# Row swaps of each batch's last two rows moved from DMA to VectorE, and ones products ahead of the first input on TensorE

**Chip, cores, metric.** One core of one Trainium2 chip. The time is the device time of one execution in microseconds (us); quoted times are medians of the fast runs, and lower is better.

## The reference

A Fourier mixing layer is followed by a two-layer network on all 24,064 tokens.

```python
X = np.fft.rfft(x, axis=1)                 # x: 8 batches x 3008 x 256
Yr = Xr @ w_r - Xi @ w_i + b_r             # mixing of the spectrum
Yi = Xr @ w_i + Xi @ w_r + b_i
Yr, Yi = soft_threshold(Yr), soft_threshold(Yi)      # lam = 0.01
y = np.fft.irfft(Yr + 1j * Yi, n=3008, axis=1)
h = np.maximum(y @ w_in, 0)                # 256 -> 2048
out = (s * h * h + b) @ w_out              # 2048 -> 256
```

## The kernel before

Transforms are products with tables: 3008 = 94 x 32 is done in two steps. Batch 0 has its own code (`first_batch`), which has nothing to hide behind. Batches 1 to 7 are transformed in small units, woven between the network's products of earlier batches. A unit of the middle steps handles one of 12 "rows" i (two pairs of spectrum blocks). Between mixing and the inverse transform, a row's 64-partition halves must change places; this is the swap. An *eviction* is the instruction of VectorE or ScalarE that copies a product's result out of its PSUM bank, so that TensorE can use the bank again; the *squaring* (`gt<-rt`) is the h * h of the network.

```python
# batches 1 to 7, row i of 12 (H = 12)
def mix_unit(i):
    ps = one_bank()                                   # one of two PSUM banks "psf"
    ...                                               # 4 products
    t, m = ring[0][:, i % 4], ring[0][:, 4 + i % 2]
    nc.vector.tensor_tensor(out=t, in0=ps, in1=..., op=ALU.add)      # the mixing sum; frees the bank
    nc.vector.tensor_tensor(out=m, in0=t, in1=low, op=ALU.max)
    nc.vector.tensor_tensor(out=m, in0=m, in1=high, op=ALU.min)
    nc.vector.tensor_tensor(out=t, in0=t, in1=m, op=ALU.subtract)
    z = ring[0][:, 6 + i % 6]
    for j in range(2):
        for r in range(2):
            nc.sync.dma_start(                        # the swap: 4 transfers of 32 KB
                out=z[64 * r : 64 * r + 64, j], in_=t[64 * j : 64 * j + 64, r]
            )

def inv_unit(i):                                      # inverse transform of row i
    ps = one_bank()
    for j in range(2):
        nc.tensor.matmul(ps[:, j, :], T_t[:, 2 * i + j, :], z[:, j, :], start=True, stop=True)
    ...

# batch 0
def first_batch():
    for c in range(4):                                # four pieces of x, as they land
        for dc in range(2):
            ...                                       # 8 products; ScalarE and VectorE evict to ut
    place_f(); place_t()                              # tables F_t, F_2, T_t copied from F_c, T_c
    gate = nc.gpsimd.tensor_copy(out=w_in_t[0][0:1, 0:1], in_=T_c[0:1, 0, 0:1])
    with tc.issue_after(gate.ins):                    # GpSimd: waits until T_c has landed
        emit_load_x(1)
        emit_load_weights()
    for i in range(...):
        mix(i); fwd_dft(i - 1); inv_dft(i - 2)        # ... and the rest of the transform
        if i == 6:
            make_w_g(); make_bounds()                 # arithmetic on GpSimd
```

## Time and profile before

| | before |
|---|---|
| median (lowest to highest, 4 runs) | 873.02 us (872.90 to 874.69) |
| span of the profiled execution | 871.1 us |
| TensorE, VectorE, ScalarE busy | 96%, 80%, 74% |
| idle of TensorE between 100 and 850 us | 8.6 us, of which 7.6 waits for swaps |
| stretches at half clock (granted clock 0.50) after 100 us, while TensorE works | 2, of 3.41 us each (127.19 to 130.61 and 236.42 to 239.84) |

A product's line in the timeline shows its start, its length, how many products were merged, and in brackets how long TensorE had been idle and what ended that. TensorE's busy share says how often it had work, not how fast it did it: the same four products take 0.60 us at full clock and 1.06 at half. The lines themselves stand in the prediction.

### The profile page before, as it was taken

To read this page: it belongs to the slowest core of one execution; us is meant where nothing else is said; L and a number is where in the kernel's file an instruction comes from. 1 tells how busy PE (TensorE), PEld (TensorE's weight loads), DVE (VectorE), ACT (ScalarE), POOL (GpSimd) and SP (SyncE) were. 2 spreads that over 40 slices of the span, in tenths; PEclk is the share of its full clock that TensorE was granted. 3 is DMA by queue.
4 is the path that set the end of the run, shared out by engine and by line. 5 is a ranking of instruction groups with operands and counts; after the bars stand their busy time and mean duration, and the time that the engine had idled before them with its cause. 6 is when DMAs were issued, how large, how long until landed. Compare 5 with 4: busy or idle time off the path is not lost.

```text
span 871.1 us, 16955 instructions
## 1 busy us (share of the span) xinstructions
PE 838.8 (96%) x6580; PEld 599.4 (69%) x6580; DVE 693.4 (80%) x971; ACT 640.7 (74%) x848; POOL 32.8 (4%) x53
## 2 busy tenths in 40 slices
PE   4889999999899999999999999999999999999996
PEld 3757766777567766777667776777667777766665
DVE  6788977888778987888878988798877887776664
ACT  4687876787677886787777787787877778666662
POOL 4100000000000000000000000000000000000000
PEclk9999999999999999999999999999999999999999
DMA  8754366423664248522764236633364133411111
GB/s 187 130 120 119 90 156 160 140 57 81 163 147 133 79 107 226 135 65 74 175 165 121 68 94 168 168 92 85 86 189 120 50 86 103 116 31 38 37 39 53
DMA packets 109346, 96.90 MB, mean 111 GB/s; under 512 B 10318, under 2 KB 101714, under 8 KB 107922
## 3 DMA queue, kind: packets, MB, share of 16 engines
q1 hardware_dynamic: 103266, 81.41, 32.6%
q0 software_dynamic: 6000, 14.42, 10.2%
q8 instruction: 51, 0.84, 0.4%
q14 instruction: 29, 0.24, 0.1%
HBM read 52.54 MB, written 46.66 MB: 114 GB/s over the span
## 4 chain that ended last, share of the span: by engine, by line
PE 89%; DMA 5%; ACT 2%; DVE 2%; issue 1%; SPq 1%; POOL 0%; DVEq 0%; POOLq 0%
PE psh L689 36%; PE psa L758 36%; PE psf L558 4%; DMA ring<-ring 3%; PE psf L493 3%; PE psf L529 2%; PE psf L544 2%; PE psf L638 2%; PE psf L585 2%; DMA x<-in_x_dram 1%; ACT rt L696 1%; DVE T_t L291 1%; PE psh L357 1%; ACT yt L158 0%; ACT m L393 0%
## 5 line engine op out<-in xcount | busy, mean ns | idle before, releaser
L696 ACT ACTIVATE rt<-psh 128x1024 f32<-128x1024 f32 (+2 forms) x384 | 386.8, 1008 | 121.3 <-PE psh L689 119.6
L703 DVE TENSOR_TENSOR gt<-rt 128x1024 f16<-128x1024 f32 (+2 forms) x322 | 385.8, 1200 | 111.2 <-ACT rt L696 110.7
L758 PE MATMUL psa<-w_out_t,gt 128*128 128x256 f16 (+1 forms) x3024 | 455.5, 273 | 0.1
L758 PEld LDWEIGHTS <-gt 128*128 128x128 f16 (+1 forms) x3024 | 301.7, 101 | 188.3 <-issue 3.6
L689 PE MATMUL psh<-yt,w_in 128*128 128x512 f16 (+1 forms) x1344 | 398.5, 379 | 0.0
L689 PEld LDWEIGHTS <-w_in 128*128 128x128 f16 x1536 | 143.2, 98 | 26.0 <-issue 1.1
L768 DVE SCALAR_TENSOR_TENSOR ost<-psa,s_bc,bias_bc 128x512 f32<-128x512 f32 (+1 forms) x96 | 70.8, 737 | 8.9 <-PE psa L758 6.1
L158 ACT CAST v<-psf 128x512 f16<-128x512 f32 x79 | 46.0, 582 | 29.0 <-PE psf L585 28.4
L700 ACT ACTIVATE gt<-rt 128x1024 f16<-128x1024 f32 (+2 forms) x62 | 65.4, 1055 | 0.9
L563 DVE TENSOR_TENSOR ring<-psf,s 128x512 f16<-128x512 f32 x84 | 57.4, 683 | 3.4 <-PE psf L558 3.3
L158 ACT CAST u<-psf 96x512 f16<-96x512 f32 x79 | 45.7, 580 | 16.5 <-PE psf L493 16.2
L158 ACT CAST xf<-psf 128x512 f16<-128x512 f32 x78 | 45.7, 585 | 10.4 <-PE psf L529 10.4
L689 PE MATMUL psh<-tail,w_in 128*128 128x512 f16 (+1 forms) x192 | 52.1, 353 | 0.0
L558 PE MATMUL psf<-W_g,xf 128*128 128x256 f16 x336 | 50.4, 273 | 0.0
L158 ACT CAST yt<-psf 128x480 f16<-128x480 f32 (+2 forms) x71 | 36.4, 526 | 10.8 <-PE psf L638 10.7
L493 PE MATMUL psf<-x,A_t 94*96 94x512 f16 x104 | 39.9, 384 | 1.1 <-ACT yt L158 0.5
L585 PE MATMUL psf<-ring,T_t 128*128 128x256 f16 x168 | 33.2, 275 | 7.7 <-DMA ring<-ring 7.6
L569 DVE TENSOR_TENSOR ring<-ring,high 128x512 f16<-128x512 f16 x84 | 35.5, 422 | 2.1
L570 DVE TENSOR_TENSOR ring<-ring 128x512 f16<-128x512 f16 x84 | 35.4, 422 | 2.0
L568 DVE TENSOR_TENSOR ring<-ring,low 128x512 f16<-128x512 f16 x84 | 35.3, 420 | 1.5
L558 PEld LDWEIGHTS <-xf 128*128 128x128 f16 x336 | 32.9, 98 | 3.7
L182 POOL DMA_DIRECT2D x<-in_x_dram x32 | 16.7, 525 | 492.3 <-PE psf L493 456.0
(77 smaller groups left out, 479.3 us busy)
## 6 DMA issues: line engine op xcount, KB each, us to landing
out_dram<-ost SPq DMA_DIRECT2D x152, 128.0 KB
x<-in_x_dram POOLq DMA_DIRECT2D x32, 376.0 KB, 6.4
ud<-u SPq DMA_DIRECT2D x28, 384.0 KB
us<-ud SPq DMA_DIRECT2D x28, 384.0 KB
ring<-ring SPq DMA_DIRECT2D x336, 32.0 KB
vd<-v SPq DMA_DIRECT2D x42, 256.0 KB
vs<-vd SPq DMA_DIRECT2D x14, 768.0 KB
out_dram<-ost SPq DMA_DIRECT2D x16, 120.0 KB
```

Of the source, the lines that this page charges most:

```text
L158: return None, nc.scalar.copy(out=dst, in_=src)
L493: nc.tensor.matmul(ps[0:96, :], A_t[0:N1, :], x16[(b, c)][0:N1, j * D : (j + 2) * D], start=True, stop=True,)
L558: nc.tensor.matmul(ps[:, r, :], xt[:, 2 - r, dc], W_g[:, dc, r], start=(dc == 0), stop=(dc == DC - 1),)
L563: nc.vector.tensor_tensor(out=t, in0=ps, in1=hold[i // 2][:, i % 2].unsqueeze(1).to_broadcast([P, 2, D]), op=ALU.add,)
L569: nc.vector.tensor_tensor(out=m, in0=m, in1=high, op=ALU.min)
L585: nc.tensor.matmul(ps[:, j, :], T_t[:, 2 * i + j, :], z[:, j, :], start=True, stop=True)
L689: nc.tensor.matmul(o, w_in_t[dc][:, mc * P : (mc + 1) * P], r, start=(dc == 0), stop=(dc == DC - 1),)
L696: nc.scalar.activation(out=rt[:, :, 0:w], in_=ps[:, :, 0:w], func=AF.Relu)
L700: nc.scalar.activation(out=gt[:, :, 0:w], in_=rt[:, :, 0:w], func=AF.Square)
L703: nc.vector.tensor_tensor(out=gt[:, :, 0:w], in0=rt[:, :, 0:w], in1=rt[:, :, 0:w], op=ALU.mult)
L758: nc.tensor.matmul(ps[0:size, h, :], gts[(ti, mc // 2)][:, mc % 2, sub * size : (sub + 1) * size], w_out_t[:, mc, :], start=(mc == 0), sto ...
L768: nc.vector.scalar_tensor_tensor(out=ost[0:size, 0:k], in0=ps[0:size, 0:k], scalar=s_bc[0:size], in1=bias_bc[0:size, 0:k], op0=ALU.mult, o ...
```

## The change

It has two parts. The swaps of rows 10 and 11, at the end of a batch, become VectorE copies. And TensorE multiplies a tile of ones while the pieces of the first x arrive, which is meant to have it at full clock when real work comes.

```diff
+    ones = cpool.tile([P, P], F16, name="ones")      # moved up
+    nc.vector.memset(ones, 1.0)
+    def keep_awake(n):
+        ps = other_bank()
+        for _ in range(n):
+            nc.tensor.matmul(ps[:, 0:P], ones, ones, start=True, stop=True)
 ...
     def first_batch():
+        keep_awake(44)
         for c in range(N2 // XCH):
             for dc in range(DC):
 ...
-                    nc.tensor.matmul(
+                    last_pe = nc.tensor.matmul(
 ...
+            with tc.issue_after(last_pe.ins):
+                keep_awake(18 if c < 3 else 12)
 ...
             for j in range(2):
                 for r in range(2):
-                    nc.sync.dma_start(
-                        out=z[64 * r : 64 * r + 64, j], in_=t[64 * j : 64 * j + 64, r]
-                    )
+                    o, a = z[64 * r : 64 * r + 64, j], t[64 * j : 64 * j + 64, r]
+                    if i < H - 2:
+                        nc.sync.dma_start(out=o, in_=a)
+                    else:
+                        nc.vector.tensor_copy(out=o, in_=a)
+                        load["dve"] += 0.13
```

`load` is the counter by which the kernel, while it is built, shares evictions between VectorE and ScalarE. The line numbers of the kernel move: the inverse product L585 is L598 after, L689 is L702, L758 is L771, and the new copy is L590.

More of the change, by code (lines that the diff above doesn't have):

```diff
@@ L244 @@
     nc.vector.memset(neg_lam, -LAM)
-    ones = cpool.tile([P, P], F16, name="ones")
-    nc.vector.memset(ones, 1.0)
     F_t = cpool.tile([P, NPAIR, P], F16, name="F_t")
```

## The prediction

> **What bounds the kernel now.** I read the page's busy shares first, then the waits, then the timeline of TensorE around each long wait, then the first 30 us on TensorE and VectorE, and last the busy times by stretch.
>
> ```profile
> PE 838.8 (96%) x6580; PEld 599.4 (69%) x6580; DVE 693.4 (80%) x971; ACT 640.7 (74%) x848; POOL 32.8 (4%) x53
> ...
> 100.00:850.00 750.00, 741.38 (x5708) 526.90 (x5706) 604.43 (x839) 563.41 (x737) 16.42 (x26) 1.00 0.42 110
> ...
> PE psf L585 <- DMA ring<-ring: 7.6, 6, 3.2
> ```
>
> TensorE (PE) is busy 96% of the span. From 100 to 850 us it idles only 750.00 - 741.38 = 8.6 us, and 7.6 us of that is one kind of wait: the inverse transform (L585) waiting for the swap of its rows, the ring<-ring transfers, 6 times, 3.2 us at the longest. Everything else in that stretch is hidden behind TensorE; VectorE (DVE) has 750 - 604 = 146 us to spare. The six waits stand in the timeline at 126.43 (2.06 us), 236.05 (3.18), 327.59 (1.21), 432.47 (0.30), 536.17 (0.48) and 536.81 (0.36): sum 7.59. Each is before the last inverse product of a batch, row i = 11 of 0 to 11 (at 432 and 536 one of its two products); batches 6 and 7 have none.
>
> The waits cost more than their length. The longest:
>
> ```profile
> 232.27 0.60 PE L758 MATMUL psa<-w_out_t,gt 128*128 128x256 f16 x4
> 236.05 0.63 PE L585 MATMUL psf<-ring,T_t 128*128 128x256 f16 x2 [3.18 <-DMA ring<-ring]
> 236.48 1.06 PE L689 MATMUL psh<-yt,w_in 128*128 128x512 f16 x2
> 237.33 1.06 PE L758 MATMUL psa<-w_out_t,gt 128*128 128x256 f16 x4
> ...
> 240.52 0.60 PE L758 MATMUL psa<-w_out_t,gt 128*128 128x256 f16 x4
> ...
> 127.20:130.60 3.40, 3.40 (x14) 1.97 (x13) 0.46 (x1) 1.74 (x3) 0.00 (x0) 0.50 0.79 208
> ...
> 236.40:239.80 3.40, 3.40 (x12) 1.68 (x13) 0.69 (x1) 0.68 (x2) 0.00 (x0) 0.50 0.47 146
> ```
>
> The same four products take 0.60 us before the wait and 1.06 after it, until about 239.8. The stretches just behind the two longest waits have a granted clock of 0.50 and carry 12 and 14 products where the 3.4 us after them carry 25. After the 1.21 us wait nothing of the kind shows: the stretch 325.2 to 328.6, where it lies, has TensorE busy 2.19 of 3.40 us (64%), and the products after it are at 0.60 again. In the two stretches before the slow ones TensorE was busy 1.34 of 3.40 (39%) and 0.33 of 3.40 (10%).
>
> The start:
>
> ```profile
> 14.29 1.46 PE L320 MATMUL psh<-A_t,x 94*128 94x96 f16 x16 [1.20 <-DMA x<-in_x_dram]
> ...
> 21.39 0.80 PE L357 MATMUL psh<-W_t,ut 128*128 128x256 f16 x3 [1.10 <-ACT g L364]
> 24.43 0.26 PE L388 MATMUL psf<-g,F_t 128*128 128x128 f16 x1 [2.25 <-DVE g L367]
> 24.50 0.31 PE L388 MATMUL psf<-g,F 128*128 128x128 f16 x1
> 24.60 0.31 PE L388 MATMUL psf<-g,F_t 128*128 128x128 f16 x1
> ...
> 16.93 0.25 DVE L285 COPY F<-F_c 64x384 f16<-64x384 f16 x1
> ...
> 18.47 4.65 DVE L291 COPY T_t<-T_c 32x1536 f16<-32x1536 f16 x4
> 23.16 1.23 DVE L367 TENSOR_TENSOR g<-psh,b_g 128x1024 f16<-128x1024 f32 x1
> ```
>
> Starts of 128-column products lie 107 ns apart at 24.5 us, and 55 ns apart from about 29 us. So TensorE runs slowly until about 28 us, though the page's clock row shows 9 there; the durations decide. But TensorE isn't what bounds this stretch. The x pieces land at 6.2, 9.1, 11.6 and 14.3 us; from 15.65 to 24.4 VectorE works with no idle (last two ut evictions, eight F copies, four T_t copies, first g), and the first forward product waits for that g.
>
> [...]107 against 55 ns, and two slow stretches whose ends in the timeline lie some 3.4 us apart. [...]The trace has the 64x384 copies at 0.25 us each, starting about 0.17 us apart, so I take 0.16 us of engine time per new copy and about 0.25 us for the last to be visible. [...]the chain's swaps take 4.4 to 7.7 us here, behind other traffic, so a copy on chip is far shorter.
>
> **Part 1, the swaps.** Rows 10 and 11 of each of 7 batches take 4 transfers each: 56 of 336 leave the queue and become 56 VectorE copies of 64x256 f16. VectorE gains 56 x 0.16 = 9 us, spread over seven places, 1.3 us each, against 146 us spare: nothing on the path. Is the copy early enough? In batch 2 the last mixing product starts at 222.05, VectorE ends that row's subtraction at 226.76, and four copies make it about 227.6 with completion. The product that waited was ready at 232.87, so 5 us remain. In batch 1 the mixing product is at 117.1 and the inverse is ready at 124.4, similar. So all six waits should go: 7.6 us. The two half-clock stretches go with them: 3.41 us each at half speed cost 3.41 x 0.5 = 1.71 us each, 3.4 us together. Nothing hides this, because TensorE has no other idle in this stretch to swallow it. Sum: 11.0 us. I take off 0.4 us for leftover short waits, since the balance counter now shifts some evictions between the engines.
>
> **Part 2, the ones products.** The ones tile is set first on VectorE (0.17 us at about 0.9), so 44 products can start at about 1.15 us. At 107 ns they last 4.7 us, until 5.9, just before x at 6.2. With the following 18 per piece (1.9 us slow, 1.0 fast) the array should run at full clock by about 8 us. They cost nothing: after the fast 16 products (about 0.7 us) and 18 more (1.0), 1.7 of the roughly 2.6 us between pieces is filled. What does it buy? ScalarE's eviction of the last piece starts 0.85 us after the piece's first product, 8 x 80 ns + about 0.2; at full clock 8 x 42 ns (the pitch of the 96-column products at 42 us) + 0.15 = 0.49. So VectorE's chain starts, and all behind it ends, 0.36 us sooner. The 16 mix products then take 1.8 instead of 3.4 us, but only to wait for VectorE: 12 extra products end before 16 us, mixing ends at about 18.3, and until about 24.1 TensorE has 3 products to do. That is almost 6 us with some 0.3 us of work, more idle than the 2.06 us that dropped the clock at 126. So I expect it slow again at 24 us, and warmed again by real work as before, at 27 to 30 us. If it stayed fast, the 4.5 us from 24.4 would shrink by at most 2.3, and VectorE and ScalarE would give some back: 1 to 2 us. I weigh that 1 in 6 and take 0.5 us for the whole part.
>
> Sum: 873.0 - 11.0 + 0.4 - 0.5 = **861.9 us**, 1.3% less.
>
> **Rivals.** (a) *The wait moves.* Row 9 still goes by transfer, and its inverse at 229.44 has no wait but perhaps little room: its issues end at 222.2, and a swap like row 11's 7.7 us would land at 229.9. For: the slack is thin in batch 2. Against: nothing before row 9 gets faster within its batch, and the queue holds fewer transfers. It would give back 1 to 3 us: 863 to 865. (b) *VectorE becomes the bound.* Copies stand in line ahead of the squaring and the output evictions. For: 80% busy. Against: no product waits for gt at all now, and 1.3 us per batch is one squaring (1.2 us). Cost under 2 us: up to 864. (c) *The transfers were hidden anyway*, the 3% that the chain of waits gives to ring<-ring being flight time beside which TensorE worked. True of most of that 3% (26 us), but the 7.6 us are real idle, so I don't count the 26. If another transfer (vd to vs, x) fell due in the same place, only the clock penalty would go: 869. Nothing waits for vs or us now. (d) *The start gains more*: 859.5 to 860.5. (e) *The ones products are in the way*: if the array is still slow at the first piece, 16 x 80 + 18 x 107 ns = 3.2 us outlasts the 2.9 us to the next piece by 0.3 us; later pieces catch up.
>
> **Range and chances.** (a) and (b) pull up by 1 to 3 us, (d) down by 1.5 to 2.5[...]. Hence 859.5 to 865.5. Faster by over 2% needs 17.5 us, more than all idle and slow clock that I can find on the path: 2%. Slower by over 2% has no mechanism of that size: 1%. Within 2%: 97%.
>
> **What would show it.** Right: no wait of L585 for ring transfers; no stretch at clock 0.50 between 100 and 850 us; VectorE up by some 9 us; copies of 64x256 at 0.2 to 0.25 us; last-piece eviction 0.3 to 0.4 us sooner; 128-column products again 107 ns apart at 24 us, the T_t copies again ahead of the first g. Wrong: waits at row 9, or products waiting for VectorE; or 55 ns already at 24 us, which would mean the start gained more than I say.

Passages that no trace of this case shows are cut out at the marks. No term of the sum is among them: 873.0 - 11.0 + 0.4 - 0.5 = 861.9. The pulls that stand give 859.4 (861.9 - 2.5) to 864.9 (861.9 + 3). The 107 and 55 ns behind the first mark are the distances between starts of 128-column products given before it. "Full clock by about 8 us" is the author's estimate; in the trace before, products that started in a row from 24.43 us on were at full pace by 29.09.

## The result

| | before | after |
|---|---|---|
| median (lowest to highest, 4 runs each) | 873.02 (872.90 to 874.69) | 861.36 us (860.90 to 862.33) |
| span of the profiled execution | 871.1 | 860.5 us |
| VectorE busy | 693.4 | 699.4 us |
| TensorE idle, 100 to 850 us | 8.6 | 1.4 us |

The ratio is 0.9863, 95% interval 0.9846 to 0.9881. A ratio here is the mean time of one kernel's fast runs over that of the other's fast runs of the same rounds, so it is not quite the ratio of the medians. The predicted time was 861.9.

First the middle stretch of the changed kernel, busy time by engine (TensorE, weight loads, VectorE, ScalarE, GpSimd, then granted clock, DMA share, GB/s), and the same for the two 3.4 us stretches which in the kernel before held the longest wait and the half clock behind it:

```profile
100.00:850.00 750.00, 748.59 (x5803) 535.24 (x5800) 619.08 (x897) 572.66 (x753) 16.87 (x26) 1.00 0.41 108
...
233.00:236.40 3.40, 3.40 (x25) 2.18 (x24) 2.77 (x3) 2.29 (x3) 0.00 (x0) 1.00 0.35 95
236.40:239.80 3.40, 3.40 (x26) 2.30 (x24) 2.66 (x3) 2.23 (x4) 0.51 (x1) 1.00 0.98 253
```

No wait for a swap is left, and no half clock from 100 us to the end of TensorE's work. The place that waited 3.18 us before is a smooth run now; these are its inverse products in TensorE's timeline:

```profile
228.89 0.38 PE L598 MATMUL psf<-ring,T_t 128*128 128x256 f16 x2
229.97 0.38 PE L598 MATMUL psf<-ring,T_t 128*128 128x256 f16 x2
```

And these are the end of the last row's arithmetic and its copies in VectorE's timeline:

```profile
224.57 0.42 DVE L580 TENSOR_TENSOR ring<-ring 128x512 f16<-128x512 f16 x1
225.02 0.97 DVE L590 COPY ring<-ring 64x256 f16<-64x256 f16 x4
```

The copies end at 226.0, 4 us before row 11's product needs them.

**Where the time came from.** I cut the traces at marks that both kernels have, the start of the first product of the network, the last inverse product of each batch (where a line of TensorE's timeline merges its two products, the start of that line) and the end of the last product. Intervals in us:

| interval up to | before | before, 2nd trace | after | after, 2nd trace |
|---|---|---|---|---|
| first product of the network | 56.60 | 58.85 | 57.98 | 56.83 |
| end of batch 1 | 71.46 | 71.53 | 68.86 | 68.87 |
| batch 2 | 107.99 | 108.69 | 103.13 | 103.14 |
| batch 3 | 91.54 | 91.10 | 88.34 | 88.33 |
| batch 4 | 104.88 | 104.90 | 104.83 | 104.82 |
| batch 5 | 104.34 | 104.67 | 103.14 | 103.15 |
| batch 6 | 99.65 | 99.65 | 99.62 | 99.62 |
| batch 7 | 101.18 | 101.18 | 101.18 | 101.17 |
| last product | 126.94 | 126.94 | 126.94 | 126.94 |

From the first product of the network on, the change saves 11.9 us in the first pair of traces, all of it in the intervals with waits and half clock. What follows batch 7 is the same to 0.01 us. The start is another matter: it varies by over 2 us from run to run, and in these traces the change does not clearly shorten it.

### The profile page after: what moved, and what is told of

The parts are those of the page before. It is cut to its first block, busy times and chain, and to the rows that moved or that the text cites. A ratio compares the mean times of both kernels' runs of the same rounds, so it can differ in the third digit from the quotient of the medians.

```text
span 860.5 us, 17125 instructions
## 1 busy us (share of the span) xinstructions
PE 839.1 (98%) x6690; PEld 604.3 (70%) x6690; DVE 699.4 (81%) x1019; ACT 642.8 (75%) x856; POOL 33.2 (4%) x53
## 4 chain that ended last, share of the span: by engine, by line
PE 89%; DVE 4%; ACT 3%; DMA 2%; issue 1%; SPq 0%; POOL 0%; DVEq 0%; POOLq 0%
PE psh L702 36%; PE psa L771 36%; PE psf L568 4%; PE psf L503 3%; PE psf L539 2%; PE psf L554 2%; PE psf L598 2%; PE psf L651 2%; DMA x<-in_x_dram 1%; DVE gt L716 1%; ACT rt L709 1%; PE psh L367 1%; DVE T_t L298 1%; ACT yt L158 1%; ACT m L403 0%
## 5 line engine op out<-in xcount | busy, mean ns | idle before, releaser
L771 PE MATMUL psa<-w_out_t,gt 128*128 128x256 f16 (+1 forms) x3024 | 453.9, 272 | 0.1
L771 PEld LDWEIGHTS <-gt 128*128 128x128 f16 (+1 forms) x3024 | 301.1, 101 | 186.9 <-issue 1.7
L702 PE MATMUL psh<-yt,w_in 128*128 128x512 f16 (+1 forms) x1344 | 396.9, 378 | 0.0
L702 PEld LDWEIGHTS <-w_in 128*128 128x128 f16 x1536 | 142.8, 98 | 26.6 <-issue 1.7
L573 DVE TENSOR_TENSOR ring<-psf,s 128x512 f16<-128x512 f32 x84 | 57.4, 683 | 3.5 <-PE psf L568 3.3
L158 ACT CAST xf<-psf 128x512 f16<-128x512 f32 x82 | 48.0, 585 | 11.1 <-PE psf L539 11.1
L702 PE MATMUL psh<-tail,w_in 128*128 128x512 f16 (+1 forms) x192 | 52.1, 353 | 0.0
L158 ACT CAST yt<-psf 128x480 f16<-128x480 f32 (+2 forms) x76 | 38.5, 518 | 14.4 <-PE psf L651 14.4
L651 PE MATMUL psf<-C_t,vs 96*128 96x96 f16 x448 | 32.9, 205 | 0.0
```

The lines of the kernel that those rows point to most:

```text
L158: return None, nc.scalar.copy(out=dst, in_=src)
L573: nc.vector.tensor_tensor(out=t, in0=ps, in1=hold[i // 2][:, i % 2].unsqueeze(1).to_broadcast([P, 2, D]), op=ALU.add,)
L651: nc.tensor.matmul(ps[:, j * 96 : (j + 1) * 96], vs[(b, h)][:, k, ec * P : (ec + 1) * P], C_t, start=True, stop=True,)
L702: nc.tensor.matmul(o, w_in_t[dc][:, mc * P : (mc + 1) * P], r, start=(dc == 0), stop=(dc == DC - 1),)
L771: nc.tensor.matmul(ps[0:size, h, :], gts[(ti, mc // 2)][:, mc % 2, sub * size : (sub + 1) * size], w_out_t[:, mc, :], start=(mc == 0), sto ...
```

## Experiments

Twelve kernels, in three groups of four; those of a group ran on one chip beside the kernel before, whose medians there were 873.67, 873.32 and 873.98 us. All gave the right result.

### 1. Each part alone

`swaps_only` is the change without all `keep_awake` calls; `awake_only` has them but leaves every swap a transfer:

```diff
# swaps_only
-        keep_awake(44)
-            with tc.issue_after(last_pe.ins):
-                keep_awake(18 if c < 3 else 12)
# awake_only
-                    if i < H - 2:
+                    if i < H:
```

> Only the swaps of rows 10 and 11 go to VectorE; no ones products. Theory (nearly all of the gain is the six waits, 7.6 us, and the two half-clock stretches behind them, 3.4 us): 873.0 - 11.0 = 862.0 us, within 1 us of the full change (861.4), no half-clock stretch after 100 us. Rival (the ones products at the start carry a part of the gain worth naming, 2 us or more): 863.5 us or above.

Measured: 862.06 us, ratio 0.986 (0.9836 to 0.9883).

> Only the ones products at the start; all swaps stay transfers. Theory (VectorE's copies bound the start, the clock falls back before 24 us): 872 to 873.5 us, the six kinds of wait for the ring transfers still there, and 128-column products again 107 ns apart at 24 us. Rival (the faster start is a gain in itself): 871 us or below.

Measured: 874.57 us, ratio 0.9988 (0.9961 to 1.0016). Its trace has 7.5 us of waits for swaps, in 8 pieces, and two half-clock stretches after 100 us.

So the swaps carry the whole change within what these runs resolve; the ones products alone are worth nothing measurable. `awake_only` came out 1.1 us above its expected range, with an interval that still holds 1. Its profiled run had a late start: one of VectorE's F copies lasted 2.80 us, and the first forward product came at 27.02 (section 4 has more of this).

### 2. What a wait costs beyond its length

The first attempt filled the wait instead of removing it: 32 ones products just ahead of row 11's inverse in batches 1 and 2 of the kernel before.

```diff
# fill_waits, on the kernel before
             z = zt.pop(i)
+            if i == H - 1 and b <= 2:
+                for _ in range(32):
+                    nc.tensor.matmul(ps[:, 0, 0:P], ones, ones, start=True, stop=True)
```

> The kernel before, with 32 products of the ones tile (128 columns, about 1.8 us at full clock) put ahead of the last inverse product in batches 1 and 2 only, into the bank that this product then overwrites. They lie inside the two longest waits, so the wait for the transfer stays and only its idle time is filled. Theory (a long wait is paid twice, the second time as 3.41 us at half clock): both half-clock stretches vanish and the time falls by 2 x 1.71 = 3.4 us to 869.6 us, although the transfers land no sooner. Rival (the half clock is hidden, or the products cost what they save): 872.5 to 874 us.

Measured: 872.43 us, ratio 0.998 (0.9958 to 1.0002): between the two theories, and not clear of zero. The trace shows that the experiment was built on an error of mine. In batch 1 the wait is not row 11's:

```profile
125.25 0.27 PE L588 MATMUL psf<-ring,T_t 128*128 128x256 f16 x1
127.59 0.28 PE L588 MATMUL psf<-ring,T_t 128*128 128x256 f16 x1 [2.07 <-DMA ring<-ring]
...
128.80 1.95 PE L586 MATMUL psf<-ones 128*128 128x128 f16 x32
130.59 0.38 PE L588 MATMUL psf<-ring,T_t 128*128 128x256 f16 x2
```

L588 is the inverse product here. TensorE waited between the two products of row 10, and the ones products came after, in front of row 11, where they only cost 1.8 us. In batch 2 they stood in the right place: no idle was left there, and no half clock followed. The trace goes further with the theory than the time does: no half clock is left after 100 us, and from the first product of the network to the end of the last product it takes 804.67 us, against 807.98 and 808.65 in the two traces of the kernel before. But in batch 1 the half clock is gone although the wait stayed, and the intervals of the times hold both no gain and the whole 3.4 us. One hit and one miss cannot settle the sum.

The next experiment, made for another question, answered it. `row11_only` is the full change with `if i < H - 1`: row 10's swaps stay transfers.

> The full change with row 11 alone copied by VectorE, row 10 left as transfers. Theory (all six waits were for row 11): the same as the full change within 1 us, 860.5 to 862.5 us. Rival (row 10's transfers are next in line and become the wait, as its inverse stands just ahead of row 11's): a wait of L598 for ring transfers appears, 1 to 5 us worse, with perhaps a half-clock stretch.

Measured: 868.29 us, ratio 0.9932 (0.9913 to 0.9952), some 7 us above the full change. The theory fell, and the rival was right and even too mild. There is one wait, row 10's in batch 1. TensorE's timeline:

```profile
130.27 0.39 PE L598 MATMUL psf<-ring,T_t 128*128 128x256 f16 x1 [3.77 <-DMA ring<-ring]
130.45 0.63 PE L503 MATMUL psf<-x,A_t 94*96 94x512 f16 x1
130.88 1.06 PE L702 MATMUL psh<-yt,w_in 128*128 128x512 f16 x2
```

Two half-clock stretches lie around and behind it (busy times by stretch, columns as above):

```profile
128.60:132.00 3.40, 1.73 (x6) 0.84 (x7) 0.00 (x0) 1.07 (x2) 0.00 (x0) 0.50 0.81 254
132.00:135.40 3.40, 3.40 (x14) 1.91 (x13) 0.93 (x2) 1.02 (x1) 0.00 (x0) 0.50 0.31 101
135.40:138.80 3.40, 3.40 (x25) 2.32 (x24) 1.91 (x2) 1.79 (x3) 0.00 (x0) 1.00 0.56 132
```

Batches 1 and 2 together take 74.09 + 104.78 = 178.87 us here and 68.87 + 103.14 = 172.01 in the second trace of the full change: 6.9 us for one wait. Of it 3.77 is the idle time. From 130.27, where work resumes, to 135.39, where the clock comes back, 5.1 us pass at half speed, worth 2.6 us. That leaves 0.5 us. A part of it is idle which the profile does not show: a product of 256 columns is drawn 0.27 us long but the next starts 0.11 us later, so some 0.16 us of every wait counts as busy. Here the wait is seen to be paid a second time with nothing else changed: the second payment is some two thirds of the first.

### 3. How many rows VectorE can take

```diff
# all_rows: if i < 0      # rows8_11: if i < H - 4
```

> The full change with all 12 rows of each batch copied by VectorE, 336 copies, no ring transfers. By the 0.22 us per copy of the changed kernel's trace, at most 62 us more of VectorE than with 56 copies, less what the balance counter moves to ScalarE: VectorE from 81% to about 87%. Theory (the copies lie in VectorE's spare time as long as it has some): 860.5 to 863 us, no wait of L598. Rival (VectorE in line order delays the squarings and evictions that TensorE needs): products of L771 or L702 wait for VectorE, 866 us or more.

Measured: 878.81 us, ratio 1.0049 (1.0027 to 1.0071), 17.7 us slower than the full change on the same chip. I had expected no loss, and the rival was right about the time, though the products that wait are not those it named. VectorE is at 85%, short of full. TensorE's timeline, with one of its new waits:

```profile
291.43 0.60 PE L568 MATMUL psf<-W_g,xf 128*128 128x256 f16 x4
...
295.57 0.60 PE L554 MATMUL psf<-W_t,xf 128*128 128x256 f16 x4 [1.58 <-DVE ring L573]
```

VectorE's work in the same moments:

```profile
292.53 0.93 DVE L590 COPY ring<-ring 64x256 f16<-64x256 f16 x4
293.49 1.23 DVE L716 TENSOR_TENSOR gt<-rt 128x1024 f16<-128x1024 f32 x1
294.63 0.28 DVE L545 TENSOR_TENSOR xf<-xf 128x256 f16<-128x256 f16 x1
294.83 0.68 DVE L573 TENSOR_TENSOR ring<-psf,s 128x512 f16<-128x512 f32 x1
```

And the largest group of these in the view of waits (total, times, longest):

```profile
PE psf L554 <- DVE ring L573: 5.6, 10, 1.6
```

The mixing products at 291.43 are done by 292.03, but their sum L573, which empties the bank, starts at 294.83, behind four copies, a squaring and an addition. Meanwhile the next row's products (L554) find no free psf bank, and TensorE idles. So what counts is not VectorE's mean load but how long a bank waits in its line. TensorE's idle from 100 to 850 us is 11.4 us there, 10.0 more than in the full change; the rest of the 17.7 us is not accounted for.

> The full change with rows 8 to 11 copied (112 copies instead of 56). With all rows copied, TensorE waited for VectorE's mixing sums, which stood behind the copies and held the two mixing banks; it cost 17 us. If that cost is in proportion to the extra copies (17 us for 280 more), 56 more cost 3.5 us: 864 to 865.5 us. If there is a threshold of VectorE's load below which the copies are free: 861 to 862.5 us.

Measured: 864.35 us, ratio 0.9894 (0.9873 to 0.9916). So the step from 56 to 112 copies is not free: it costs some 3 us, as the proportion to `all_rows` said. Whether the first 56 cost anything was not tested. Two waits for L573 stand in the trace (0.84 and 1.26 us). By copied rows per batch the times are 868.3 (one), 861.1 to 861.4 (two), 864.4 (four) and 878.8 (twelve), so two is the best of those tried. Fewer leaves a transfer late, more makes banks wait.

### 4. What sets the start

`after_again` is the full change once more; the other two edit it.

```diff
# pool_later: GpSimd's second set of work waits for the T_t copies, not for their source
-        gate = nc.gpsimd.tensor_copy(out=w_in_t[0][0:1, 0:1], in_=T_c[0:1, 0, 0:1])
+        gate = nc.gpsimd.tensor_copy(out=w_in_t[0][96:97, 0:1], in_=T_t[96:97, 0, 64:65])
 ...
             if i == 6:
-                make_w_g()
-                make_bounds()
+                with tc.issue_after(gate.ins):
+                    make_w_g()
+                    make_bounds()
# warm_gap
+            if i == 1:
+                keep_awake(76)
             if 0 <= i - 1 < 2 * U:
                 fwd_dft(*steps[i - 1])
```

> The full change once more, to be compared with the next three on one chip. 861 to 862 us.

Measured: 861.14 us, ratio 0.9856 (0.9831 to 0.9881).

> The full change, with 76 more ones products (4.2 us at full clock) in the idle time ahead of the first forward product, where the clock fell back in the full change. Theory (the start is set by VectorE, so full clock there buys 1 to 2 us at most, part of it taken back by VectorE and ScalarE): 128-column products 55 ns apart from the first forward product on, 859.5 to 861 us. Rival (slow TensorE sets the 24 to 31 us stretch): 3 us or more gained, 858.5 us or less.

Measured: 859.92 us, ratio 0.984 (0.9816 to 0.9864). The clock stays full from 4.7 us to the end of the work, and from the first forward product to the network it takes 30.68 us instead of 31.88 (`after_again`): 1.2 us, as the theory said and as the medians show, though the ranges overlap (859.34 to 861.99 against 860.95 to 864.27). In the first trace of the full change, where the half clock at this place lasted 6.83 us and not 3.41, this stretch took 33.02 us. So a slow TensorE costs 1.2 to 2.3 us of this stage and does not set it.

> The full change, with GpSimd's second set of work (issue of the next x and of the weights, then its arithmetic on W_g and the bounds) held back until the T_t copies are written instead of until their source has landed. Theory (VectorE's F and T_t copies set the start, and they are slow because GpSimd works beside them): the four T_t copies fall from 4.65 us in sum to about 1.9 us [...], the first forward product starts 2.5 to 3 us sooner, and the time falls by 1.5 to 3 us to about 859 us. Rival (the copies are slow by themselves, from their 32 partitions or the stride): their time stays and the time is the same or a little worse through later weights.

Measured: 857.58 us, ratio 0.9809 (0.9783 to 0.9834), 3.6 us under the full change on the same chip. VectorE's T_t copies in the full change (first trace):

```profile
19.00 4.65 DVE L298 COPY T_t<-T_c 32x1536 f16<-32x1536 f16 x4
23.68 1.23 DVE L377 TENSOR_TENSOR g<-psh,b_g 128x1024 f16<-128x1024 f32 x1
```

The same in this kernel:

```profile
18.96 2.24 DVE L298 COPY T_t<-T_c 32x1536 f16<-32x1536 f16 x4
21.24 1.22 DVE L377 TENSOR_TENSOR g<-psh,b_g 128x1024 f16<-128x1024 f32 x1
```

And its first forward products on TensorE:

```profile
22.52 0.22 PE L398 MATMUL psf<-g,F_t 128*128 128x128 f16 x1 [1.27 <-DVE g L377]
22.57 0.22 PE L398 MATMUL psf<-g,F 128*128 128x128 f16 x1
```

The same copies take 0.55 us each when GpSimd rests (2.24 us for the four, where the estimate was 1.9) and up to 1.67 beside its work, so GpSimd was lengthening VectorE's path at the start. The first forward product comes 2.4 us sooner, at 22.52 against 24.95, and by then the clock has not fallen back: starts 55 ns apart, and 30.59 us from there to the network against 31.88. The two together are the 3.7 us by which the network starts sooner (53.11 us against 56.83 in `after_again`), more than the 1.5 to 3 us expected. The edit moved GpSimd's DMA issues, the transfers they start and its arithmetic together, so which of the three slows a copy is not shown. `swaps_only` has a longer delay of this kind. There a copy that takes 0.25 us elsewhere in the same line lasted 2.89:

```profile
17.66 0.25 DVE L292 COPY F<-F_c 64x384 f16<-64x384 f16 x1
...
18.10 2.89 DVE L292 COPY F<-F_c 64x384 f16<-64x384 f16 x1
```

This explains most of why the start varies. In three traces (`swaps_only`, `awake_only`, `before_again`) one F copy lasts 2.8 to 2.9 us, and the first forward product comes at 26.02 to 27.02; in the eight others with GpSimd's work in its old place no F copy does, and it comes at 24.43 to 25.22.

### 5. On from there

```diff
# later_no_awake: pool_later without all keep_awake calls
# tt_after_g: pool_later, with place_t() and the gate moved behind the first g
+            if i == 1:
+                with tc.issue_after(g_last[0].ins):
+                    place_t()
+                gate = ...; emit_load_x(1); emit_load_weights()
```

> GpSimd's second set of work held back behind the T_t copies, swaps of rows 10 and 11 on VectorE, but no ones products. Theory (once VectorE's path at the start is short, the gap of TensorE before 22 us is too short for the clock to fall back, so the ones products now pay: in the held-back run the clock was full from 4.6 us on): without them TensorE is slow until 25 to 29 us and the time is 1 to 3 us longer than the held-back run's 857.6, 858.6 to 860.5 us. Rival (the ones products are idle decoration at any length of VectorE's path): 857 to 858.2 us.

Measured: 858.45 us, ratio 0.9823 (0.9803 to 0.9844), against 857.58 and 0.9809 with the ones products on another chip. The difference of 0.9 us is just below the expected 1 to 3, and the intervals overlap, so the worth of the ones products is indicated here, not shown. The traces show two effects that work against each other: without the ones products, products are 107 ns apart until 26.2 us and the stretch from the first forward product to the network takes 32.34 us instead of 30.59, but the last piece of x is in work at 14.47 us instead of 15.41.

> The held-back kernel (with ones products), with the T_t copies moved behind the first g on VectorE; they are needed only by the inverse product. Theory (VectorE's line sets the start): the first forward product starts as soon as g and the F_t copies of ScalarE are done, near 20.3 us instead of 22.5; the copies then stand ahead of the first z, so of these 2 us some 1 us is left at the end: 856 to 857.3 us. Rival (the T_t copies only change places in one line): 857.3 to 858.5 us.

Measured: 856.02 us (855.39 to 857.00), ratio 0.9799 (0.9779 to 0.9819). The first forward product is at 20.71, and this version beats both kernels: 18 us under the one before on its chip, and by the ratios (0.9799 against 0.9863 and 0.9856) some 5 us under the change.

> The kernel before, profiled a second time, to see how much its waits and its start vary from run to run: waits of L585 for the ring transfers of 6 to 10 us in sum, at least one half-clock stretch behind the longest, start of the first forward product between 24 and 27 us, 871 to 877 us.

Measured: 876.70 us, one run. Its waits for swaps sum to 7.5 us again, with two half-clock stretches, and the first forward product comes at 26.02 instead of 24.43. Here too an F copy lasted 2.79 us. The middle of the kernel repeats well; the start does not.

## Why the prediction was right

The time was predicted as 861.9 and is 861.4, and most steps held as written. Point by point:

- **The waits.** All are gone, as said. But not all belonged to row 11: in batch 1 it was row 10's (`fill_waits`, `row11_only`). The step "each is before the last inverse product of a batch" failed. It did not matter to the number, because the change copies both rows; it did matter to two experiments. The mistake was to name rows by position without counting the four inverse products at the end of each batch.
- **Paid twice.** Right for the two longest of the six waits, as said. Both half-clock stretches vanished, and `row11_only` shows a wait and its half clock added up in the interval times.
- **The sum of part 1.** The 11.0 us (10.6 after the deduction) was too small: the intervals after the start give 11.9. The missing 0.9 fits the idle that products drawn 0.27 us long hide, 6 x 0.16 = 1.0 us by estimate. The deduction for leftover short waits wasn't needed.
- **The copies.** VectorE was to gain 9 us; it gained 6.0, and ScalarE 2.1, because the counter moved work over: VectorE has 48 instructions more, not 56, and ScalarE 8. A copy was mis-sized: four take 0.92 to 0.98 us, so 0.24 each, not 0.16 (the median length of one is 222 ns). I had taken the pitch of the F copies for them. The margin in batch 2 was 4.0 us, not 5.
- **Part 2.** The mechanism was right: the clock is full from 6.6 us, falls back at 23.6, products are 107 ns apart at 25.0, and VectorE's line with the T_t copies ahead of g decides. Between the last piece's first product and ScalarE's eviction of it 0.30 us is saved (0.85 to 0.55), where 0.36 was said. What failed is the 0.5 us of gain in all, which `awake_only` doesn't show: the last piece itself starts later, at 15.27 instead of 14.29. It does so in all nine traces with ones products (15.06 to 15.95) and in none of the five without (14.29 to 14.67). The x transfer is what is late: it was issued at 2.87 us in both kernels and landed at 15.23 instead of 14.24, and TensorE stood waiting for it. Why it lands later is open.
- **Rivals.** (a) the wait moves to row 9, and (b) VectorE becomes the bound: neither at this dose. At four and twelve rows (b) is what happens, by a way I hadn't named: held banks, not late squarings. (c) the transfers were hidden anyway: no, TensorE's idle fell from 8.6 to 1.4 us. (d) the start gains more: not in the change, but 3.6 us were there once GpSimd was moved, and perhaps 1 more with T_t out of the way (0.9809 against 0.9799 on another chip, intervals overlapping). (e) the ones products are in the way: no, TensorE waited for the x transfer before each of the four pieces (3.7 us in all).

In the total, a part 1 too small by 1.3 us (11.9 against 10.6) and a gain of part 2 of 0.5 us that the traces do not show partly cancel. With a start that varies by 2 us on top, the hit to 0.5 us is in part luck.

## What to carry to other kernels

A short wait on TensorE is to be priced with the half-clock time that may follow it (in `row11_only` 3.77 us of idle, then 5.1 us of work at a granted clock of 0.50): look for a granted clock of 0.50 and for longer products after the wait. When work is moved to an engine with spare time on average, ask which results already stand in its line and which buffers they hold (in `all_rows` VectorE was 85% busy, and TensorE still waited up to 1.6 us for a sum behind its copies); the best dose here was the two rows with waits, and more was worse. And when an engine's copies take several times their own minimum (the T_t copies up to 1.67 us against 0.55), look at what its neighbour does in those microseconds before making the copies fewer.

## What these runs leave open

- What makes the clock drop. Before: a 3.4 us stretch 39% busy was followed by half clock, one 64% busy was not. In `fill_waits` a stretch 44% busy (1.50 of 3.40 us) was not either. But in `awake_only` one 45% busy (1.53 of 3.41 us, from 14.13) was followed by half clock, and in `row11_only` even one 69% busy (2.37 of 3.41 us, from 50.05). So TensorE's busy share alone does not decide it, and no limit can be read off these runs.
- How long one copy of VectorE can last beside GpSimd's work. In `swaps_only` a copy that takes 0.25 us elsewhere ran from 18.10 to 20.99, while GpSimd went from issuing the load of w_out_t (18.38, 1.20 us) to its W_g arithmetic (19.58, 1.29 us): longer than either of them, as far as GpSimd's spans, which are rough, can be trusted.
- Why the last piece of x comes about 1 us later beside ones products: its first product starts at 15.06 to 15.95 us in nine traces with them, at 14.29 to 14.67 in five without.
